# Mixture-of-experts stage: four small moves of work on VectorE, GpSimd and in the buffers

## The chip, the cores and the metric

The kernel runs on one core of a Trainium2 chip. The metric is the device time of one execution in microseconds, the median of several runs. The profile is that of one further execution, taken by the hardware profiler.

## The reference

Three stages follow one another; the output of each is the input of the next. The sizes are 2 batches of 576 tokens, so 1152 tokens of 512 values, all in float32.

```python
# 1. attention, 8 heads of 64, with rotary positions on q and k
scores = (1 / np.sqrt(64)) * np.matmul(q_rot, k_rot.transpose(0, 1, 3, 2))
attn = softmax(scores)                      # over the last axis
x = np.matmul(attn, v)                      # then to (1152, 512)
# 2. dense feed-forward, 512 -> 2048 -> 512
h = x @ w_in
x = np.maximum(0.01 * h, h) @ w_out
# 3. eight experts, 512 -> 1024 -> 512, the two best of each token
logits = x @ w_gate
noisy_logits = logits + np.log1p(np.exp(x @ w_noise)) * noise
top2 = two largest noisy_logits of a token; top2_w = softmax over the two
for e in range(8):
    for k in range(2):
        mask = top2[:, k] == e
        h = np.maximum(x[mask] @ w1[e], 0.0)
        out[mask] += top2_w[mask, k, None] * (h @ w2[e])
```

## The kernel before

The change touches only the third stage. Each expert gets a fixed block of `C` = 320 rows, in three groups of 128, 128 and 64. A branch at the end (`tc.If(crowded > C)`, line 1298) handles an expert with more rows; it is not taken here. Each float32 operand is split into a high half (`fp32r`) and a low half, the rest; a product takes three matmuls: high by high, high by low, low by high. `xe[e]` is the pair of rows of expert e, `xe_h` and `xe_l`, 4 x 320 values in each of 128 partitions.

**Units.** An expert is cut into eight units f of 128 hidden values. A unit is `expert_mm1` (12 matmuls of line 599, then `relu`, lines 1139 to 1141: ScalarE writes the high half `g_x` or `g_y`, VectorE its low half) and `expert_mm2` (eight matmuls, lines 1158 to 1162, into three banks `yr`). The loop runs over n = 8e + f. An iteration first issues `expert_mm1` and `relu` of a later unit (the next one for n below 9, the one after next from then on), then the side work of the unit, then `expert_mm2` of its own unit, then `refill`, which splits two weight blocks for a unit twelve later (lines 217 on ScalarE and 219 on VectorE) and issues the loads of further ones on SyncE. In this stage the order of work on TensorE, VectorE, ScalarE and GpSimd is the order in which the program issues it; each engine works its queue in order.

**From routing to rows.** For expert e, `row(e)` (line 740, VectorE) makes numbers and gates of the tokens, `onehot(e, js)` (line 938, VectorE) makes one-hot columns `hot`, one instruction for each of nine groups of tokens, and `table(e)` (line 950) multiplies the two in nine small matmuls on TensorE. VectorE then makes row numbers and gates of it (lines 958 to 967), and `gather(e)` (line 978) fetches the rows: ten indirect DMAs on GpSimd's queue into the tile `got`. `turn(e, f)` does what follows in four steps at the units that `TURN` gives: `turn_x(e, 0)` turns the first half of `got` on VectorE (line 988) and writes its `xe_h` on ScalarE (line 990), `low_x(e, 0)` writes its `xe_l` on VectorE (line 999), and the same again for the second half. In iteration (e, f) the program works on the rows of expert e + 1 and on `row`, `onehot` and `table` of expert e + 2: `row` at f = 4, columns 0 to 4 at f = 5, columns 5 to 8 at f = 6, the table and the gather at f = 6 too, behind the columns. For e = 0 `row` and the columns come at f = 2 and 3.

**The first expert.** Its rows are not gathered by a table: `rows` (lines 808 to 814) copies the last three blocks of 128 tokens into `x1_row` tiles and stores them to memory by SyncE; 24 matmuls at line 1110 put the expert's rows into four banks `xk`; ScalarE (line 1123) and VectorE (line 1121) write `xe_h` from there, two banks each, VectorE the four pieces of `xe_l` (line 1125), and the `opening` matmuls (line 1233) begin the experts.

**Addresses.** The pool `moe2_x` has two buffers for each name; the first tile of a name gets buffer 0, the next buffer 1, and so on in turn. The pool is laid over memory that has just come free. Counted down from the upper end of a partition, in bytes, buffer 0 of `xe_h` lies at 33,536 to 38,656 and buffer 1 at 28,416 to 33,536. Of what lay there before, `x1` took 12,288 to 30,720, `gx` 30,720 to 36,864 and the three `x1_row` tiles 36,864 to 43,008. A writer of a new tile waits for the users of what lay at its address.

**The end.** `put_y(e, st)` scales a group of an expert's results (`scale_y`) and adds it to `out` by an indirect DMA on GpSimd (`add_y`, line 1191): 24 scatter-adds in all. Those of the last expert stand behind the branch. With the 70 gathers and three of the first expert (line 1036), GpSimd issues 97 indirect DMAs. The program ends (line 1391) when SyncE has waited for all transfers and every engine has run its closing drains.

Of the kernel before, what the change touches and what calls it, by code (L numbers as in the profile page):

```python
# [11 lines left out]
F32R = mybir.dt.float32r  # L12
# [11 lines left out]
E, FF2 = 8, 1024  # L24
# [5 lines left out]
C = 320  # L30
# [50 lines left out]
def f32(t):  # L81
    return t.bitcast(F32)
# [3 lines left out]
def fused_kernel(ctx, tc, q, k, v, w_in, w_out, w_gate, w_noise, noise, w1, w2, consts, out):  # L86
    nc = tc.nc
    V, A, G, T = nc.vector, nc.scalar, nc.gpsimd, nc.tensor

    def pool(name, bufs=1, **kw):  # L90
        return tc.tile_pool(name=name, bufs=bufs, reuse_waits="tile", **kw)
# [231 lines left out]
    def turn(pr, n, a, at=None):  # L323


        r = roped[pr, n][0]
        if pr == 0:
            if at is None:
                p = aside.append(ps_o.tile([128, 1024], F32, name="pT", tag="o")) or aside[0]
            else:  # L330
                p = ps(at, "pT", (128, 1024))
            turned[pr, n, a] = p
            for j in range(KT):
                if a == 0:
                    T.transpose(p[:64, j * 128:(j + 1) * 128], r[:, j, 0], ident)
                else:
                    T.transpose(p[:, j * 128:(j + 1) * 128], r[:, j].rearrange("p h d -> p (h d)"), ident)
            return
        p = ps(at, "pT")
        for j in range(KT):  # L340
            for w in range(2):
                T.transpose(p[:, w, j * 64:(j + 1) * 64], r[here(w), j].rearrange("p h d -> p (h d)"), ident[here(w), here(w)])  # L342
        turned[pr, n, a] = p[:, :, :KT * 64].rearrange("p w (j n) -> p j w n", n=64)
# [394 lines left out]
    def row(e, J=slice(0, NJ), a=0, z=5):  # L738
        n, t = parts(e), row2[e % 2] if e else row0
        V.tensor_tensor(t[:, J, :, a:z], sel[:, J, e, :n, None].to_broadcast([128, J.stop - J.start, n, z - a]),  # L740
                        load[:, J, e, None, a:z].to_broadcast([128, J.stop - J.start, n, z - a]), op=OP.mult)
# [194 lines left out]
    def onehot(e, js):  # L936
        for j in js:
            V.tensor_scalar(hot[e % 2][:, j], iota_32 if e else iota_b, BIG, place[:, j, e:e + 1], op0=OP.add, op1=OP.is_equal)
# [6 lines left out]
    def table(e, bk, a=0, z=5):  # L945

        w, n = z - a, parts(e)
        t = bk[:, :n * w].rearrange("p (a b) -> p a b", b=w)
        for j in range(NJ):
            T.matmul(t, hot[e % 2][:, j], (row2[e % 2] if e else row0)[:, j, :, a:z], start=(j == 0), stop=(j == NJ - 1))  # L950
        whole = nc.allow_low_precision(reason="whole numbers")
        if e == 0:
            with whole:
                V.tensor_reduce(idx[e], t[:, :, 0:2], axis=AX.X, op=OP.add)
            V.tensor_reduce(gates[e], t[:, :, 2:5], axis=AX.X, op=OP.add)
            return
        if a == 0:
            V.tensor_reduce(found[:, 0, :n], t[:, :, 0:2], axis=AX.X, op=OP.add)
            V.tensor_scalar(chunks[e - 1], found[:, 0, :n], 4.0, const("quad"), op0=OP.mult, op1=OP.add)
        if z == 5:  # L960
            V.tensor_reduce(found[:, 1, :n], t[:, :, 2 - a:5 - a], axis=AX.X, op=OP.add)
            m = tmp.tile([128, 2, 3, 4], F32, name="found_here")
            V.tensor_tensor(m, found.rearrange("p w (s q) -> p w s q", q=4),
                            const("mine")[:, None, None, :].to_broadcast([128, 2, 3, 4]), op=OP.mult)
            with whole:
                V.tensor_reduce(idx[e], m[:, 0], axis=AX.X, op=OP.add)
            V.tensor_reduce(gates[e], m[:, 1], axis=AX.X, op=OP.add)
# [4 lines left out]
    got, xe = {}, {}  # L972

    def gather(e):

        got[e] = m2.tile([128, NB32 * 128], F32, name="got", bufs=1)
        for b in range(NB32):
            G.indirect_dma_start(out=got[e][:, b * 128:(b + 1) * 128], out_offset=None,  # L978
                                 in_=x1_rows.rearrange("n (q c) -> (n q) c", q=4),
                                 in_offset=bass.IndirectOffsetOnAxis(ap=chunks[e - 1][:, b:b + 1], axis=0))  # L980
# [119 lines left out]
    for i in range(3):  # L1100
        t = gpool.tile([128, 2 * C + 64], F32R, name="g_x", bufs=3)
# [13 lines left out]
    m2 = m2stack.enter_context(pool("moe2", bufs=2, side="right"))  # L1115
    m2xstack = ExitStack()
    m2x = m2xstack.enter_context(pool("moe2_x", bufs=2, side="right"))
    xe[0] = [m2x.tile([128, 4, C], F32R, name=f"xe_{t}") for t in "hl"]
    for k in range(4):
        if k % 2:  # L1120
            V.tensor_copy(xe[0][0][:, k], xk[k][:, :C])
# [22 lines left out]
    def expert_mm1(e, f, between=None):  # L1144
        h = hb[(8 * e + f) % 3]
        mm1(c0 + 8 * e + f, h, xe[e], 0, C, between)
        return relu(h)
# [3 lines left out]
    def expert_mm2(e, f, g, sts=(0, 1, 2)):  # L1151

        hi, lo = slots[(c0 + 8 * e + f) % NSLOT]
        hi, lo = hi[:, 1], lo[:, 1]
        for st in [st for st in sts if st < 2]:
            gh, gl = (g[:, o + 128 * st:o + 128 * st + 128] for o in (0, C))
            for t, (s, w) in enumerate(((gh, hi), (gh, lo), (gl, hi))):
                T.matmul(yr[st], s, w, start=(f == 0 and t == 0), stop=(f == 7 and t == 2))  # L1158
        if 2 not in sts:
            return  # L1160
        T.matmul(yr[2], g[:, 2 * C - 64:], hi, start=(f == 0), stop=(f == 7), skip_group_check=True)  # L1161
        T.matmul(yr[2][:64], g[:, C - 64:C], lo, start=False, stop=(f == 7), skip_group_check=True)  # L1162
# [35 lines left out]
    def put_y(e, st):  # L1198
        r = scale_y(e, st)
        G.memset(spacer, 0.0)  # L1200
        add_y(e, st, r)
# [4 lines left out]
    def refill(c, most):  # L1206

        for p in range(nxt_part[0], min(2 * c, last_part[0], nxt_part[0] + most)):
            while nxt_part[1] <= p + 5:
                load_part(nxt_part[1])  # L1210
                nxt_part[1] += 1
            convert(p, 4)
            convert(p, 5)
            nxt_part[0] += 1
# [5 lines left out]
    def busiest(bk):  # L1220

        for i in range(NJ - T1 + 1):
            T.matmul(bk[:1, :E], one_b[:, :1], chosen[:, T1 + i] if T1 + i < NJ else chosen0, start=(i == 0),
                     stop=(T1 + i == NJ))
        V.tensor_copy(count, bk[:1, :E])
        V.tensor_reduce(most, count, axis=AX.X, op=OP.max)
# [11 lines left out]
        table(1, bank[1], 0, 2)  # L1238
        gather(1)

    TURN = {1: (4, 5, 5, 6)}

    def turn(e, f):

        for (do, part), at in zip(((turn_x, 0), (low_x, 0), (turn_x, 1), (low_x, 1)), TURN.get(e, (1, 2, 3, 4))):
            if f == at:
# [3 lines left out]
    for n, (e, f) in enumerate(seq[:-3]):  # L1250
        while len(gs) < n + (2 if n < AHEAD2 else 3):
            gs.append(expert_mm1(*seq[len(gs)], second if n == 1 else None))
        if (e, f) == (0, 0):
            r1[7]()
            r1[9]()
            r1[8](1, 0, 2)
            onehot(1, last)
        if (e, f) == (0, 1):
            r1[6]()
            r1[8](1, 2, 5)  # L1260
            r1[8](0)
            onehot(0, last)
        if (e, f) == (0, 2):
            table(1, bank[1], 2, 5)
            table(0, bank[5])
        if e + 1 < E:
            turn(e + 1, f)
        if (e, f) == (0, 7):
            busiest(bank[5])
        if e + 2 < E:  # L1270
            if f == (4 if e else 2):
                row(e + 2)
            for i in range(2):
                if f == (5 if e else 2) + i:
                    onehot(e + 2, range(5 * i, 5 + 4 * i))
        if f == 6 and e + 2 < E:
            table(e + 2, bank[1])
            gather(e + 2)
        expert_mm2(e, f, gs[n])
        if f == 7:  # L1280
            for st in range(3):
                put_y(e, st)
        if n:
            refill(c0 + n + NSLOT, 2 if n > 1 else 4)

    crowded = nc.values_load(most, min_val=0, max_val=NT)
    e = E - 1
# [10 lines left out]
    with tc.If(crowded > C):  # L1298
        with ExitStack() as rest:
# [13 lines left out]
            with tc.For_i(0, E, 1) as e:  # L1313
                n = nc.values_load(nparts[:, bass.ds(e, 1)], min_val=0, max_val=8)
                with tc.If(n > 0):
# [4 lines left out]
                    with tc.For_i(0, n, 1):  # L1320
# [4 lines left out]
                        t = bank[4][:CO, :5]  # L1325
# [68 lines left out]
```

## Time and profile before

| | |
|---|---|
| timed, median of 3 runs | 635.39 us (634.35 to 635.54) |
| the profiled execution's own time | 629.85 us |
| its span, first to last instruction | 628.0 us |
| around the span | 1.85 us |
| TensorE matmuls busy | 601.9 us (96%), 4720 instructions |
| VectorE, ScalarE, GpSimd busy | 428.5, 295.7, 248.8 us |
| mean granted clock of TensorE | 0.993 |

PE is TensorE's matmul, PEld its weight load, DVE VectorE, ACT ScalarE, POOL GpSimd, SP SyncE. Times count from the first instruction. A line such as L599 is the line of the kernel. In a timeline the number in brackets is how long the engine sat idle before the instruction, and who released it; a timeline row can merge several instructions of one kind (x4). An `x` before a number counts instructions.

### The profile page before, as it was taken

What the parts mean: (1) busy time and instruction counts of PE and PEld (TensorE: products, weight loads), DVE (VectorE), ACT (ScalarE), POOL (GpSimd) and SP (SyncE); (2) the same over time, 40 slices, a digit from 0 to 9 for tenths busy, and PEclk for the clock granted to TensorE, in tenths of its full rate; (3) what the DMA queues carried; (4) which work ended last, traced back from release to release, by engine and by line L of the source; (5) the groups of instructions that cost most, each with busy time, mean ns of one, the idle gap of its engine ahead of it and who ended that gap; (6) DMA issues with size and microseconds to landing.
All of it is one profiled execution on the core that took longest, in us unless ns stands there. A gap on an engine that the chain in (4) does not pass through costs nothing.

```text
span 628.0 us, 12453 instructions
## 1 busy us (share of the span) xinstructions
PE 601.9 (96%) x4720; PEld 503.5 (80%) x4721; DVE 428.5 (68%) x902; ACT 295.7 (47%) x605; POOL 248.8 (40%) x248
## 2 busy tenths in 40 slices
PE   8999999999999999999999989999999999999991
PEld 4666767777888888897999888898878787878881
DVE  6987887874998888623577568856666666666411
ACT  2555565765545444322244434554545444445311
POOL 6999898456200000100001007463636464646202
PEclk9999999999999999999999999999999999999997
DMA  6510422322568634902943425475757484748303
GB/s 191 161 42 21 119 64 83 87 83 89 152 201 265 205 116 139 301 1 49 276 111 119 161 50 151 146 198 156 196 157 201 151 206 147 208 147 217 53 5 42
DMA packets 83214, 85.84 MB, mean 137 GB/s; under 512 B 12365, under 2 KB 64973, under 8 KB 83150
## 3 DMA queue, kind: packets, MB, share of 16 engines
q1 hardware_dynamic: 76878, 73.82, 38.0%
q0 software_dynamic: 5392, 10.49, 8.5%
q8 instruction: 38, 0.62, 0.4%
q10 hardware_dynamic: 880, 0.69, 0.4%
q14 instruction: 26, 0.21, 0.1%
HBM read 69.96 MB, written 14.98 MB: 135 GB/s over the span
## 4 chain that ended last, share of the span: by engine, by line
PE 86%; DVE 5%; POOL 2%; issue 2%; DMA 1%; ACT 1%; SPq 0%; POOLq 0%; DVEq 0%; ACTq 0%
PE bank L599 31%; PE bank L608 16%; PE bank L1158 13%; PE pS L418 6%; PE pO L435 6%; PE pM L369 3%; PE bank L1162 2%; PE pO L451 2%; PE bank L1161 2%; POOL got L978 2%; DVE half L381 1%; PE bank L748 1%; PE pT L342 1%; PE bank L1233 1%; PE bank L950 1%
## 5 line engine op out<-in xcount | busy, mean ns | idle before, releaser
L978 POOL DMA_INDIRECT got<-x_rows,chunks x70 | 77.5, 1107 | 115.0 <-issue 76.6
L219 DVE TENSOR_TENSOR wl<-raw,wh 128x512 fp32r<-128x512 f32 x128 | 82.6, 684 | 18.6 <-ACT wh L217 18.6
L599 PE MATMUL bank<-xe_l,wh 128*128 128x320 f32 x248 | 77.0, 310 | 0.8 <-DVE xe_l L999 0.8
L599 PE MATMUL bank<-xe_h,wl 128*128 128x320 f32 x248 | 76.9, 310 | 0.0
L599 PE MATMUL bank<-xe_h,wh 128*128 128x320 f32 x248 | 76.8, 310 | 0.0
L217 ACT ACTIVATE wh<-raw 128x512 fp32r<-128x512 f32 x128 | 74.3, 626 | 0.4 <-DMA raw<-in_moe_w 0.4
L422 ACT ACTIVATE p<-pS 128x576 f32<-128x576 f32 x80 | 49.2, 651 | 40.2 <-PE pS L418 38.7
L1158 PE MATMUL bank<-wh,g_x 128*128 128x512 f32 x192 | 68.1, 395 | 0.0
L620 ACT ACTIVATE g_t<-bank 128x512 f32<-128x512 f32 (+2 forms) x48 | 23.6, 491 | 94.5 <-PE bank L599 93.6
L608 PE MATMUL bank<-g_h,wh 128*128 128x512 f32 (+2 forms) x192 | 65.2, 340 | 0.0
L599 PE MATMUL bank<-xh,wh 128*128 128x512 f32 (+2 forms) x192 | 65.0, 339 | 0.0
L599 PE MATMUL bank<-xh,wl 128*128 128x512 f32 (+2 forms) x192 | 65.0, 338 | 0.0
L608 PE MATMUL bank<-g_l,wh 128*128 128x512 f32 (+2 forms) x192 | 64.8, 338 | 0.0
L599 PE MATMUL bank<-xl,wh 128*128 128x512 f32 (+2 forms) x192 | 64.8, 337 | 0.0
L608 PE MATMUL bank<-g_h,wl 128*128 128x512 f32 (+2 forms) x192 | 64.5, 336 | 0.0
L381 DVE TENSOR_REDUCE half<-pM 128x2 f32<-128x640 f32 x70 | 51.5, 754 | 16.9 <-PE pM L369 16.2
L621 DVE TENSOR_TENSOR g_f<-bank,g_t 128x512 f32<-128x512 f32 (+2 forms) x48 | 26.8, 557 | 46.1 <-ACT g_t L620 45.6
L1139 ACT ACTIVATE g_x<-bank 128x320 fp32r<-128x320 f32 x48 | 21.0, 438 | 73.9 <-PE bank L599 70.2
L1191 POOL DMA_INDIRECT out<-y_row,idx x24 | 40.7, 1694 | 38.2 <-DVE y_row L1172 18.8
L1141 DVE SCALAR_TENSOR_TENSOR g_x<-bank,g_x 128x320 fp32r<-128x320 f32 x48 | 23.4, 488 | 41.0 <-ACT g_x L1140 41.0
L599 PEld LDWEIGHTS bank<-xe_h,wh 128*128 128x128 f32 x248 | 46.8, 189 | 5.7
L599 PEld LDWEIGHTS bank<-xe_h,wl 128*128 128x128 f32 x248 | 46.7, 188 | 2.8
(250 smaller groups left out, 1442.0 us busy)
## 6 DMA issues: line engine op xcount, KB each, us to landing
raw<-in_moe_w SPq DMA_DIRECT2D x128, 256.0 KB
raw<-in_moe_w_in SPq DMA_DIRECT2D x16, 512.0 KB
raw<-in_moe_w_out SPq DMA_DIRECT2D x16, 512.0 KB
inv_sum<-inv_sums SPq DMA_DIRECT2D x16, 144.0 KB
out<-none SPq DMA_DIRECT2D x9, 256.0 KB
VF<-in_v SPq DMA_DIRECT2D x8, 256.0 KB
kept<-wh SPq DMA_DIRECT2D x4, 512.0 KB
kept<-wl SPq DMA_DIRECT2D x4, 512.0 KB
```

The costliest lines, as they stand in the source:

```text
L217: A.activation(hi[:, part], t, AF.Copy)
L219: V.tensor_tensor(lo[:, part], t, f32(hi)[:, part], op=OP.subtract)
L381: V.tensor_reduce(halves[pr, i][:, :, j], p[:, :, :(320, 256)[i]], axis=AX.X, op=OP.max, negate=True)
L418: T.matmul(p[:, a, 0:288], w[here(a)], x[here(a), cols], start=(t == 0), stop=(t == 3))
L422: A.activation(t, scored.pop((pr, j, z))[:, :, 0:288], AF.Exp, scale=0.125)
L435: T.matmul(y[r, z, 0:288], w[:, 32 * c:32 * c + 32], prob[pr, j, z][:, a], start=(j == 0), stop=False, skip_group_check=True)
L599: T.matmul(h[:, :n], w[:, 0, k * 128:(k + 1) * 128], m[:, k, cols:cols + n], start=(i == 0), stop=(i == 11))
L608: T.matmul(b[:, o:o + n], w[:, 1, ds], m[:, :n], start=(first and opens and t == 0), stop=(last and t == 2), skip_group_check=True)
L621: V.tensor_tensor(g[:, :n], h[:, :n], t[:, :n], op=OP.max)
L978: G.indirect_dma_start(out=got[e][:, b * 128:(b + 1) * 128], out_offset=None, in_=x1_rows.rearrange("n (q c) -> (n q) c", q=4), in_offset= ...
L1158: T.matmul(yr[st], s, w, start=(f == 0 and t == 0), stop=(f == 7 and t == 2))
L1191: s = G.indirect_dma_start(out=out, out_offset=bass.IndirectOffsetOnAxis(ap=idx[e][:r.shape[0], st:st + 1], axis=0), in_=r, in_offset=None ...
```

## The change

The rows of the first expert go into the second buffers of `xe_h` and `xe_l`: two tiles `unused` are taken first, and GpSimd writes one element of each. The last step of `turn` for expert 1, `low_x(1, 1)`, is issued at unit 5 instead of 6, right behind `turn_x(1, 1)` and ahead of the unit's weight splits. From e = 1 on, `row` and the one-hot columns come one unit sooner, at f = 3, 4 and 5; the table stays at f = 6. GpSimd gets a drain at unit 3 of the last expert.

```diff
-    xe[0] = [m2x.tile([128, 4, C], F32R, name=f"xe_{t}") for t in "hl"]
+    unused, xe[0] = ([m2x.tile([128, 4, C], F32R, name=f"xe_{t}") for t in "hl"] for _ in range(2))
+    for t in unused:
+        G.memset(f32(t)[:1, 0, :1], 0.0)
...
-    TURN = {1: (4, 5, 5, 6)}
+    TURN = {1: (4, 5, 5, 5)}
...
+        if (e, f) == (E - 1, 3):
+            G.drain()
         if e + 2 < E:
-            if f == (4 if e else 2):
+            if f == (3 if e else 2):
                 row(e + 2)
             for i in range(2):
-                if f == (5 if e else 2) + i:
+                if f == (4 if e else 2) + i:
                     onehot(e + 2, range(5 * i, 5 + 4 * i))
```

## Rows read from the trace of the kernel before

**Rows 1.** The chain of waits from 340 us, shares by line.
```profile
by line: PE bank L599 37.0%; PE bank L1158 27.4%; PE bank L1162 4.5%; PE bank L1161 4.3%; POOL got L978 4.2%; PE bank L608 3.8%; issue 2.0%; PE bank L1233 1.3%; PE bank L950 1.3%; POOL out L1191 1.1%; DMA got<-x_rows,chunks 0.9%; DVE g_x L1
```

**Rows 2.** Stretch, busy us of each engine, clock, DMA share, GB/s.
```profile
440.00:560.00 120.00, 115.00 (x655) 101.18 (x654) 81.47 (x183) 58.30 (x138) 61.47 (x62) 1.00 0.64 180
```

**Rows 3.** TensorE's waits from 340 us: total, times, longest.
```profile
PE bank L950 <- DVE hot L938: 6.3, 5, 1.3
```

**Rows 4.** Timeline, first expert's rows: start, us, what, idle before.
```profile
366.85 1.92 PE L1110 MATMUL bank<-g_x,xl 128*128 128x320 f32 x12
...
369.29 0.77 ACT L1123 ACTIVATE xe_h<-bank 128x320 fp32r<-128x320 f32 x2 [3.38 <-DMA x_rows<-x_row]
...
369.77 0.42 PE L1233 MATMUL bank<-xe_h,wh 128*128 128x320 f32 x1 [1.01 <-ACT xe_h L1123]
...
370.11 1.67 DVE L1125 TENSOR_TENSOR xe_l<-bank,xe_h 128x320 fp32r<-128x320 f32 x4
```

**Rows 5.** Timeline round the second expert's rows.
```profile
395.20 0.84 DVE L988 STREAM_TRANSPOSE got<-got 128x640 f32<-128x640 f32 x1 [0.17 <-DMA got<-x_rows,chunks]
...
396.08 0.74 ACT L990 ACTIVATE xe_h<-got 128x640 fp32r<-128x640 f32 x1 [2.46 <-DVE got L988]
...
396.43 0.40 PE L950 MATMUL bank<-row,hot 128*128 128x50 bf16 x9
...
396.67 0.48 PE L1158 MATMUL bank<-wh,g_x 128*128 128x512 f32 x1
...
397.37 1.29 DVE L219 TENSOR_TENSOR wl<-raw,wh 128x512 fp32r<-128x512 f32 x2 [1.32 <-ACT wh L217]
...
398.58 0.48 DVE L1141 SCALAR_TENSOR_TENSOR g_y<-bank,g_y 128x320 fp32r<-128x320 f32 x1
...
398.98 0.81 DVE L999 TENSOR_TENSOR xe_l<-got,xe_h 128x640 fp32r<-128x640 f32 x1
...
399.85 0.41 PE L599 MATMUL bank<-xe_l,wh 128*128 128x320 f32 x1 [0.79 <-DVE xe_l L999]
...
401.69 0.50 PE L1158 MATMUL bank<-wh,g_y 128*128 128x512 f32 x1
```

**Rows 6.** Timeline round the table of expert 3, one of five alike.
```profile
428.83 0.30 PE L950 MATMUL bank<-row,hot 128*128 128x50 bf16 x5
...
429.67 0.49 DVE L1141 SCALAR_TENSOR_TENSOR g_x<-bank,g_x 128x320 fp32r<-128x320 f32 x1 [1.10 <-ACT g_x L1140]
...
430.07 0.73 DVE L938 TENSOR_SCALAR hot<-iota,place 128x128 bf16<-128x128 bf16 x4
...
430.90 0.48 PE L1158 MATMUL bank<-wh,g_x 128*128 128x512 f32 x1
...
431.10 0.18 DVE L958 TENSOR_REDUCE found<-bank 128x10 f32<-128x20 f32 x1 [0.29 <-PE bank L950]
...
432.33 1.29 POOL L978 DMA_INDIRECT got<-x_rows,chunks  x1 [11.95 <-issue]
```

**Rows 7.** VectorE's timeline in units 4 and 5 of expert 1.
```profile
423.72 0.62 DVE L740 TENSOR_TENSOR row<-sel,load 128x450 bf16<-128x450 bf16 x1
...
426.47 0.90 DVE L938 TENSOR_SCALAR hot<-iota,place 128x128 bf16<-128x128 bf16 x5
```

**Rows 8.** Groups of GpSimd's DMAs; line 1391's drains (ns, start); last scatters.
```profile
L978 POOL DMA_INDIRECT got<-x_rows,chunks x70 | 77.5, 1107 | 115.0 <-issue 76.6
L1191 POOL DMA_INDIRECT out<-y_row,idx x24 | 40.7, 1694 | 38.2 <-DVE y_row L1172 18.8
...
L1391 POOLq DRAIN  x3: 46/113/9648, 617.5 to 627.7; - x3
L1391 SPq DRAIN  x3: 7/7/13, 622.8 to 627.4; - x3
...
613.65 1.56 POOL L1191 DMA_INDIRECT out<-y_row,idx  x1 [18.80 <-DVE y_row L1172]
617.75 1.42 POOL L1191 DMA_INDIRECT out<-y_row,idx  x1 [0.67 <-DVEq L1298]
```

## Prediction

> **What bounds the kernel now.** I read the chain of waits first: from 340 us to the end it runs almost wholly through TensorE, and its longest links are the matmuls of the experts, lines 599 and 1158 [rows 1]. The table of stretches says the same of 440 to 560 us: TensorE is busy 115.00 of 120 us at a granted clock of 1.00, VectorE 81.47, ScalarE 58.30 [rows 2]. What a change is worth here is therefore the time in which TensorE stands still, and what comes after its last matmul. The list of TensorE's waits names 6.3 us in five stops for the one-hot columns `hot` of the tables [rows 3]; the timeline has two more, 1.01 us once for `xe_h` of the first expert [rows 4] and 0.79 once for `xe_l` of the second [rows 5]. All three are touched. After the last matmul the end is set elsewhere, by GpSimd [rows 8], and that is the fourth part.
>
> **First rows in the other buffer.** The first write of `xe_h` waits for the DMA that stores the last `x1_row` tiles: ScalarE sat idle 3.38 us until 369.29 [rows 4]. The reason is an address: buffer 0 of `xe_h` lies over the pool of those tiles, buffer 1 over `x1` and `gx`, which are read long before. With buffer 1 the writers need only the banks. The matmuls that fill these (24 at line 1110) end at 366.85 + 1.92 = 368.77; the banks close one after the other, two matmuls apart, so the first piece of `xe_h` can be written while the last six still run. TensorE can go on at about 368.77 instead of 369.77, which is its whole idle time of 1.01 [rows 4]. What is late next is `xe_l`: four pieces in 1.67 us [rows 4], from about 369.3 to 371.0, wanted from about 12 matmuls after the start on, 370.6 to 371.1. That just fits. The two one-element memsets on the unused buffers now take over the wait for the store (to 369.2); GpSimd has nothing to do until the gather of expert 1, which hangs on TensorE's table and moves forward with it. Bounds: 0, if buffer 1 waits for something too, and 1.01; I take 1.0.
>
> **Second expert's low half.** Today VectorE turns the second half of expert 1's rows at 395.20, ScalarE writes `xe_h` at 396.08 for 0.74, and `xe_l` comes only at 398.98, behind two weight splits and a rectifier's low half, and TensorE waits 0.79 for it [rows 5]. With the step at unit 5 instead of 6, `xe_l` is the next thing in VectorE's queue: it can start when ScalarE is through, at 396.08 + 0.74 = 396.82, and is done by 397.7. TensorE wanted it at 399.85 - 0.79 = 399.06, after the first part at about 398.06. Even if the gather did not move forward at all with TensorE, it is there in time. The price: VectorE then waits for ScalarE with two weight splits and the rectifier's low half `g_y` of unit 7 queued behind it. It stands idle there today too, 1.32 us until the splits at 397.37 [rows 5], so they move by 0.3 only and the low half ends near 399.4 instead of 399.06 (398.58 + 0.48). TensorE takes it up at 401.69 today [rows 5], at 399.9 after both gains: covered, by 0.5 us if nothing of the first part reaches VectorE and by 1.5 if all does. Bounds 0 and 0.79; I take 0.8, since the step stands earliest in the queue.
>
> **One-hot columns a unit sooner.** This is the large term. At each table TensorE runs five of the nine table matmuls at 428.83, then stops; VectorE does a rectifier's low half at 429.67 and only behind it the last four one-hot columns, 430.07 for 0.73, and line 1158 goes on at 430.90: 2.07 us from the first table matmul to the next useful one [rows 6]. The table of expert 2, whose columns are made early already, shows the same nine matmuls without a stop: 396.43 to 396.67, 0.24 us [rows 5]. So each stop costs 2.07 - 0.24 = 1.83 us, more than the idle time listed for it, because the last four matmuls follow the columns one by one. Five tables (experts 3 to 7; five stops in rows 3) make 5 x 1.83 = 9.15 us. The lower bound is the idle time alone, 6.3 us; the upper one 9.15. I take 9.15, by the row of the same operation without a stop.
>
> What hides the moved work: nothing is added, `row` (0.62) moves from unit 4 to unit 3, five columns (0.90) from 5 to 4, four from 6 to 5 [rows 7]. Unit 3 has a turn of `got`, behind which VectorE stands idle for ScalarE as at expert 1, 1.32 us [rows 5], so `row` fills a hole; unit 4 gets 0.3 more than it has, unit 5 less. VectorE is busy two thirds of the stretch [rows 2]. Without that cover a late low half would have to eat a lead of two units of TensorE before a matmul waited. Next in line is the gather: today it starts at 432.33, some 1.2 us after the first reduction of the table at 431.10 [rows 6]. The reduction can then follow the low half directly, at 430.1, so the gather comes 1.0 us sooner, while TensorE comes 1.83 sooner: the gather loses 0.8 us against it, per expert but not adding up, as each expert starts anew from its table. What it has in hand is not in a row of its own; VectorE's only wait for a gather in all experts is the one of 0.17 us at expert 1 [rows 5], so 0.8 us that were missing would first show as such a wait on VectorE, ahead of the lead of two units.
>
> **GpSimd drained in the last expert.** The last three scatter-adds end with a drain on GpSimd's queue that takes 9648 ns, from 617.5 to 627.2, while the other two of its drains there take 46 and 113 ns and SyncE's three 7 to 13 [rows 8]. The last scatter's descriptors are out at 617.75 + 1.42 = 619.17, and SyncE, which waits for the landing of every scatter, comes to its own drain at 622.8 [rows 8]. From 622.85 to 627.17 the core waits for GpSimd's drain alone: 4.3 us. What sets its length no row shows directly. Behind it stand 70 gathers and 24 scatters [rows 8] and three gathers for expert 0 with no drain between: 8.0 us after the last issue over 97 is 0.08 us each (an estimate from these rows). If the drain works off what all of them left, a drain in the last expert leaves three, and the last one ends before SyncE's: gain 4.3. If it is a fixed price after any scatter, the gain is 0. Those are the bounds. I take 4.3, since the two drains that have no indirect DMA before them are the nearest rows to a drain with little behind it. The new drain itself stands behind expert 6's scatters; GpSimd then idles 18.80 us until the last ones [rows 8], so 9.65 us fit, with the register load and branch behind it.
>
> The Trainium skill ("VectorE: DVE Perf Modes", The DRAIN you can't avoid) says that the drains of preamble and postamble take some 12 ns, constant, on all five engines. The row of SyncE agrees (7 to 13 ns); GpSimd's drains differ, this one by a factor of 800. By that rule the 9.65 us would not be the drain's own work, an earlier drain would do nothing, and the sum would be the first rival's.
>
> **The sum.** 1.0 + 0.8 + 9.15 + 4.3 = 15.25 us, made on the profiled execution: 629.85 (span 628.0 and 1.85 around it) becomes 614.6. The timed runs lie 5.5 us above that execution with the same program; I leave that difference as it is: 635.39 - 15.25 = 620.1.
>
> **Rivals.**
> (1) The end stays GpSimd's. The last drain costs the same after three scatters as after 97: for it speaks that no row shows a drain behind only a few indirect DMAs, against it the 46 and 113 ns. The gain is 10.95, the time 624.4.
> (2) Another wait takes the stop's place: the tables still wait for VectorE, now for what stands at the head of its queue, and TensorE goes on only when the low half is through at 430.07 instead of 430.90. The five stops then give 5 x 0.83 = 4.2 instead of 9.15, and the time is 625.1. Against it: the last column is then issued before that low half, and VectorE works in order.
> (3) Slower. The drain in the last expert takes GpSimd beyond its idle time: the last three scatters are queued behind it. It decides from 18.80 us on; to lose the 10.95 us and 1.3 more, the drain would have to last about 31 us, three times the longest that was seen, and the time would be over 636.7. Nothing speaks for it but that a drain in the middle was never seen.
> (4) Buffer 1 of `xe_h`, or the gather of expert 1, waits for something that is hidden now: one or both of the small terms are gone, 621.1 to 621.9.
>
> **How the numbers follow.** Chances: the forecast 0.69, (1) 0.18, (2) 0.06, (4) 0.04, (3) 0.03. The range goes from 618.5 (the forecast less what repeated runs scatter, and a few tenths where the small terms do more) to 625.6, which takes in (1), (2) and (4). Within 0.2%, 1.3 us, is about what a measurement of this kernel cannot tell from no change. Faster by more than that: everything but (3) and a failing of the large term and the drain together, 0.95; the same 0.02; slower 0.03.
>
> **What would show it.** The waits for `hot` gone from TensorE's list and nine table matmuls in about 0.25 us at each expert; the opening matmul of line 1233 with no DMA ahead of `xe_h`, 1 us sooner; `xe_l` of expert 1 right behind its `xe_h` and no wait at line 599; a drain of some 8 us in the idle time of GpSimd near 600 us and a last one so short that SyncE's drain comes last. It would be wrong if TensorE's stops came back under another name (a gather's landing, `g_x`), or if the last drain kept its 8 us.

## The result and the profile after

The changed kernel takes 614.07 us (median of 5 runs, 613.45 to 614.28) beside 635.39 for the kernel before (5 runs, 634.35 to 637.68): a ratio of 0.9651, 95% interval 0.9632 to 0.967. The gain is 21.3 us; forecast were 15.25 and a time of 620.1, and 614.07 lies below the range. The profiled execution tells another story: 614.23 us after, 629.85 before, a gain of 15.6, and the sum made on it said 614.6. The mechanism and the sum held where they were worked out. What failed is the step from the profiled execution to the timed runs.

TensorE's waits from 340 us in the kernel after (total, times, longest); `hot`, `xe_h` and `xe_l` of [rows 3 to 5] are gone, and these two rest, which are there before as well:

```profile
PE bank L1110 <- ACT x_row L808: 0.8, 1, 0.8
PE bank L887 <- DVE chosen L873: 0.2, 1, 0.2
```

The stretch of [rows 2] in the kernel after (busy us of each engine, granted clock, DMA share, GB/s): TensorE is busy 120.00 of 120 us, where it was 115.00.

```profile
440.00:560.00 120.00, 120.00 (x695) 106.49 (x694) 86.32 (x193) 64.55 (x151) 69.44 (x67) 1.00 0.67 190
```

The timeline of the kernel after at the first expert's rows (start, us, what, idle before and releaser), against [rows 4]. ScalarE and VectorE are released by the banks, not by the DMA; line 1235, which is line 1233 before, begins at 368.64 instead of 369.77. The last four matmuls shown, for `xe_l`, take 0.99 us because VectorE's four pieces only just keep ahead of them. The memset on the unused buffer waits for the store in their place.

```profile
366.88 1.92 PE L1110 MATMUL bank<-g_x,xl 128*128 128x320 f32 x12
367.96 1.02 ACT L1125 ACTIVATE xe_h<-bank 128x320 fp32r<-128x320 f32 x2 [2.02 <-PE bank L1110]
...
368.64 0.31 PE L1235 MATMUL bank<-xe_h,wh 128*128 128x320 f32 x1
...
369.25 1.68 DVE L1127 TENSOR_TENSOR xe_l<-bank,xe_h 128x320 fp32r<-128x320 f32 x4
369.36 0.09 POOL L1120 MEMSET xe_h<- 1x1 f32 x1 [22.62 <-DMA x_rows<-x_row]
...
370.40 0.99 PE L1235 MATMUL bank<-xe_l,wh 128*128 128x320 f32 x4
```

VectorE and ScalarE of the kernel after at the second expert's rows, against [rows 5]: `xe_l` at line 999 follows its `xe_h` 0.78 us later and is done by 396.4, ahead of the weight splits and of `g_y`; TensorE has no wait there.

```profile
393.94 0.85 DVE L988 STREAM_TRANSPOSE got<-got 128x640 f32<-128x640 f32 x1
394.81 0.74 ACT L990 ACTIVATE xe_h<-got 128x640 fp32r<-128x640 f32 x1 [2.35 <-DVE got L988]
...
395.59 0.83 DVE L999 TENSOR_TENSOR xe_l<-got,xe_h 128x640 fp32r<-128x640 f32 x1 [0.81 <-ACT xe_h L990]
396.33 1.29 DVE L219 TENSOR_TENSOR wl<-raw,wh 128x512 fp32r<-128x512 f32 x2
...
397.53 0.48 DVE L1143 SCALAR_TENSOR_TENSOR g_y<-bank,g_y 128x320 fp32r<-128x320 f32 x1
```

TensorE and VectorE of the kernel after round the table of expert 3, against [rows 6]: nine table matmuls without a stop, 0.24 us to the next useful one, and the reduction right behind the low half. The unit, from its first matmul of line 599 to that of the next, takes 3.94 us; before it took 5.78 (five alike).

```profile
426.62 0.40 PE L950 MATMUL bank<-row,hot 128*128 128x50 bf16 x9
426.86 0.48 PE L1160 MATMUL bank<-wh,g_x 128*128 128x512 f32 x1
...
427.46 0.49 DVE L1143 SCALAR_TENSOR_TENSOR g_x<-bank,g_x 128x320 fp32r<-128x320 f32 x1 [1.26 <-ACT g_x L1142]
427.87 0.17 DVE L958 TENSOR_REDUCE found<-bank 128x10 f32<-128x20 f32 x1
```

The drains of the kernel after (shortest, median, longest in ns; first and last start in us), against [rows 8]: the new one at line 1273, then GpSimd's and SyncE's at the end (line 1395, 1391 before). GpSimd's longest is 4911 ns instead of 9648 and ends at 611.1. SyncE comes to its drains at 611.6, so the end now waits for SyncE.

```profile
L1273 POOLq DRAIN  x1: 10795/10795/10795, 580.4 to 580.4; - x1
...
L1395 POOLq DRAIN  x3: 46/113/4911, 606.2 to 612.2; - x3
L1395 SPq DRAIN  x3: 7/7/13, 611.6 to 611.9; - x3
```

### The profile page after: what moved, and what is told of

The parts are those of the page before. It is cut to its first block, busy times and chain, and to the rows that moved or that the text cites. A ratio compares the mean times of both kernels' runs of the same rounds, so it can differ in the third digit from the quotient of the medians.

```text
span 612.5 us, 12458 instructions
## 1 busy us (share of the span) xinstructions
PE 598.7 (98%) x4720; PEld 502.0 (82%) x4721; DVE 428.9 (70%) x902; ACT 294.4 (48%) x605; POOL 252.8 (41%) x250
## 4 chain that ended last, share of the span: by engine, by line
PE 93%; DVE 4%; issue 1%; ACT 1%; POOL 1%; POOLq 0%; DVEq 0%
PE bank L599 34%; PE bank L608 16%; PE bank L1160 14%; PE pS L418 7%; PE pO L435 6%; PE pM L369 3%; PE bank L1164 2%; PE bank L1163 2%; PE pO L451 2%; PE pW L532 1%; DVE half L381 1%; PE bank L748 1%; PE pT L342 1%; PE bank L1235 1%; PE bank L1110 1%
## 5 line engine op out<-in xcount | busy, mean ns | idle before, releaser
L978 POOL DMA_INDIRECT got<-x_rows,chunks x70 | 82.2, 1174 | 77.8 <-ACT wh L217 45.1
```

## Experiments

The kernels below were timed in six sets (the first four experiments are the first set), each set on one chip and with the kernel before in it. Ratios are against the kernel before of the same set, with a 95% interval. In the six sets it took 629.93, 629.57, 630.06, 629.83, 632.09 and 629.95 us. A median like the result's 635.39 never came back.

**The kernel before, once more** (no edit).

> The kernel before, unchanged, to see its spans run by run. The profiled execution of before took 629.85 us, its timed ones 634.4 to 637.7; the changed kernel's profiled execution and its timed ones agree (614.2 and 613.5 to 614.3). Theory E (the end): GpSimd's last drain is of varying length, 9.65 us in the profile and some 15 in the others. Theory R (expert 1's rows): the gather of expert 1 lands later in other executions and TensorE waits some 6 us for it instead of 0.8. Theory S (stops): the five stops at the tables are longer in other executions by about 1.1 us each. Theory O: it lies outside what the change touches. All expect spans of some 632 to 634 in most runs and a minority near 628; if the profile falls on a longer one, its extra 5 us stand in the drain (E), ahead of line 599 near 399 us (R), at the tables (S), or elsewhere (O).

629.93 us (629.41 to 630.24, 11 runs), span 628.3. Its profile is [rows 3], [rows 6] and [rows 8] again. No run was of the longer kind, so the four theories are not tested by it. The profiled execution's 629.85 is the usual time of this kernel, and the 5.5 us on top are what has to be explained.

**The drain alone.**

```diff
+        if (e, f) == (E - 1, 3):
+            G.drain()
```

> The kernel before with the drain in the last expert alone. E: 635.4 - 4.2 - 5.5 = 625.7, with spans that no longer vary. R, S and O: 635.4 - 4.2 = 631.2. If the drain is a fixed price after any scatter (rival 1 of the prediction): 635.4.

625.73 us (625.55 to 625.8), ratio 0.9931 [0.9918, 0.9945]: 4.20 less. GpSimd's drains at its end:

```profile
L1393 POOLq DRAIN  x3: 46/113/5002, 617.5 to 623.6; - x3
```

**The columns alone.**

```diff
-            if f == (4 if e else 2):
+            if f == (3 if e else 2):
                 row(e + 2)
...
-                if f == (5 if e else 2) + i:
+                if f == (4 if e else 2) + i:
```

> The kernel before with the one-hot columns a unit sooner alone. S: 635.4 - 9.2 - 5.5 = 620.7. E, R and O: 635.4 - 9.2 = 626.2.

620.8 us (620.15 to 621.27), 0.9853 [0.9838, 0.9869]: 9.13 less, and no wait for `hot`. This time and that of the drain alone agree with a line of their forecasts (S here, E there) by luck: both lines start from 635.4 and take off a hidden 5.5 us, and here the kernel before stood at 629.93, without them. What the two runs show is the terms, 4.20 and 9.13.

**All but the drain** (the change without its `G.drain()`).

```diff
-        if (e, f) == (E - 1, 3):
-            G.drain()
```

> The changed kernel without the drain in the last expert. E: 614.1 + 9.7 = 623.8 and a last drain that varies. R, S: 614.1 + 4.2 = 618.3. O: 614.1 + 4.2 = 618.3, or 5 us more in a part of its runs.

618.75 us (618.08 to 619.1), 0.9821 [0.9808, 0.9834]: 11.18 less, with a last drain of 9650 ns. With the 4.2 of the drain that is 15.4.

**The changed kernel, once more** (no edit).

> The changed kernel unchanged, timed beside the kernel before on one chip, where the kernel before took 629.93 us. Theory B (base): the four terms are as summed, 15.3 us, and only the 635.39 us from which they were taken off is not this kernel's time on this chip: 614.5 and a ratio near 0.976. Theory H (hidden): the kernel before has some 5.5 us more to lose that only part of its executions show, and the changed kernel is free of it: 614.1 against runs of before that reach 634 to 638, ratio 0.965.

614.17 us (613.16 to 614.47) beside 629.57, 0.9751 [0.9738, 0.9764]: 15.4 less, as theory B has it. The kernel after has the time of the result; the kernel before is 5.8 us faster than there.

**The buffer and the low half without the rest**, then **each by itself**.

```diff
-    xe[0] = [m2x.tile([128, 4, C], F32R, name=f"xe_{t}") for t in "hl"]
+    unused, xe[0] = ([m2x.tile([128, 4, C], F32R, name=f"xe_{t}") for t in "hl"] for _ in range(2))
+    for t in unused:
+        G.memset(f32(t)[:1, 0, :1], 0.0)
...
-    TURN = {1: (4, 5, 5, 6)}
+    TURN = {1: (4, 5, 5, 5)}
```

> The kernel before with the other buffer and the sooner low half alone. B: 1.1 + 0.8 = 1.9 us, 628.0 beside 629.9, no wait for xe_h or xe_l on TensorE's list, the five stops for hot and the drain of 9.65 us as before. H, if what is hidden sits at expert 1's rows: as B on a chip where before takes 629.9, but 628 against 635 where it takes that.

> The kernel before with the first rows in the other buffer alone, timed beside the kernel before once more. B (only the base of the sum was off): before near 629.7, this 1.1 us less, 628.6; the wait of 0.8 us for xe_l stays, as gather and TensorE move forward together. H (some executions of before are 5.5 us longer): runs of before at 634 to 638 among these; if what is long sits at the first expert's rows, this kernel has none of it.

> The kernel before with the second expert's low half at unit 5 alone. The prediction's term: 0.8 us less than before, no wait at line 599 for xe_l. A rival: xe_l is not what sets line 599, and the wait moves to another tile with no gain. Base: before near 629.8 (B) or at 634 to 638 (H).

Both: 627.88 us, 0.9969 [0.9958, 0.998], 1.7 less. The buffer: 628.78, 0.998 [0.9971, 0.9989], 1.3 less; the wait for `xe_l` stays at 0.7. The low half: 629.13, 0.9989 [0.998, 0.9998], 0.7 less; that wait is gone and the one for `xe_h` stays at 1.0. Each small term is there by itself; the intervals are wide beside them (0.7 to 1.8 us for the buffer, 0.1 to 1.3 for the low half), and it is the waits that tell them apart.

**The drain earlier**, at unit 3 of expert 4, with 32 indirect DMAs between it and the last drain instead of three.

```diff
-        if (e, f) == (E - 1, 3):
+        if (e, f) == (4, 3):
```

> The changed kernel with its drain at unit 3 of expert 4 instead of the last expert: 32 indirect DMAs (20 gathers, 12 scatters) stand between it and the last drain instead of 3. If the last drain works off what each DMA since the drain before has left (5.0 us past the last landing for 97, so 0.05 each): 1.6 us past the landing, which SyncE's own ten waits cover by 0.6, so 614.1 + 1.0 = 615.1. If any earlier drain makes the last one short: 614.1. If only one in the idle time of the last expert does: 618.4.

614.54 us (614.22 to 615.02), 0.9758 [0.9743, 0.9773]. Its last drains:

```profile
L1395 POOLq DRAIN  x3: 46/113/5852, 606.5 to 612.9; - x3
L1395 SPq DRAIN  x3: 7/7/13, 611.7 to 612.6; - x3
```

The time is 0.4 us above the 614.17 of its set, between two lines of the forecast; the drain's length decides. It lasts 4.9 us behind 3 indirect DMAs, 5.9 behind 32 and 9.65 behind 97: from 32 to 97 it is 3.80 / 65 = 0.058 us for each. The two drains put into the experts fit in as well. The last scatter is still being issued when a drain begins; counted from the end of that issue, the drains end 3.25, 4.19, 6.25, 7.75 and 8.00 us later, behind 3, 32, 65, 94 and 97 DMAs. With 3, most of it is the landing of the last scatter, whose last packet ends 2.75 us after the issue. The drain works off what all of them left; it is no fixed price.

**Single profiled executions** of the kernel before, twice, and the kernel after once more (no edit).

> The kernel before once more, with its profile, in case its runs here are the longer ones. B: 630 and the same rows. H: if 634 to 638, the trace names the place of the extra 5 us.

> The kernel before, one profiled look in the same call. B: 630. H: 634 to 638 with the extra time in a row that can be named.

> The changed kernel beside before on whatever chip this call gets. B: 614.2 beside 629.8. H: 614.2 beside 634 to 638.

629.75 and 629.45 us, and 614.26 (two runs) beside 629.83. None was of the longer kind.

**The 5.5 us: both kernels again, in more runs** (no edit).

> The kernel before, unchanged, on whatever chip this call gets, for its spread alone. B: 629.2 to 630.7 as in the four calls so far (chips 0, 9 and 13). H, or a chip on which it is slower: 634 to 638, with a trace of it.

> The changed kernel on the same chip. B: 614.2. If the chip were a slower one for both: 619. H: 614.2 beside 634 to 638.

Here the kernel before showed a part of it: 632.17 us (629.74 to 633.56, 12 runs) and 632.09 (629.27 to 634.31, 17 runs), each run with its own granted clock, 0.992 at 629.27 and 0.988 at 633.56. Of the 29 runs the six with 0.992 or more took 629.27 to 631.14 us, the four with 0.988 or less 632.75 to 634.21. The kernel after stood at 614.3 (613.75 to 614.85, clock 0.995 to 0.997), 0.9718 [0.9688, 0.9749]: 17.8 us less. And one execution of the kernel before, of 632.28 us, was profiled. The last table's unit and the unit after it, in that execution (columns as in [rows 2]; the granted clock is the third number from the end, 0.84 and 0.87):

```profile
551.91:559.14 7.23, 5.67 (x31) 4.47 (x30) 6.25 (x23) 1.59 (x5) 1.29 (x1) 0.84 0.55 182
559.14:563.25 4.11, 4.11 (x21) 3.69 (x20) 0.77 (x2) 1.24 (x3) 3.18 (x4) 0.87 0.62 178
```

The same two units in the profile of the kernel before's first repeat (an execution of 630.03 us):

```profile
551.59:557.35 5.76, 4.51 (x30) 3.71 (x29) 4.26 (x17) 1.59 (x5) 0.48 (x1) 1.00 0.52 171
557.35:560.98 3.63, 3.63 (x21) 3.21 (x20) 1.27 (x3) 1.24 (x3) 2.72 (x4) 1.00 0.54 156
```

Together 11.34 instead of 9.39 us. TensorE's timeline of the 632.28 us execution shows why: it stops 1.56 us for the columns, and a little later its matmuls take half as long again, 0.63 us at line 1158 instead of 0.40, 0.47 at line 599 instead of 0.31, until 560.2.

```profile
555.61 0.69 PE L950 MATMUL bank<-row,hot 128*128 128x50 bf16 x4 [1.56 <-DVE hot L938]
...
556.45 0.40 PE L1158 MATMUL bank<-wl,g_x 128*128 128x512 f32 x1
...
557.43 0.63 PE L1158 MATMUL bank<-wl,g_x 128*128 128x512 f32 x1
...
559.67 0.47 PE L599 MATMUL bank<-xe_l,wh 128*128 128x320 f32 x1
...
560.20 0.32 PE L599 MATMUL bank<-xe_h,wl 128*128 128x320 f32 x1
```

From 558 to 560 us of that execution the granted clock is 0.50, the lower of its two levels, 1.2 GHz:

```profile
558.00:560.00 2.00, 2.00 (x8) 1.60 (x7) 0.56 (x1) 0.00 (x0) 1.70 (x2) 0.50 0.26 36
```

The columns come late because VectorE does, and VectorE because ScalarE does. Once in each of five experts ScalarE waits long before `g_x`, although its bank was full, each time 9 to 10 us ahead of a table's unit:

```profile
417.58 0.44 ACT L1139 ACTIVATE g_x<-bank 128x320 fp32r<-128x320 f32 x1 [2.94 <-PE bank L1162]
...
448.95 0.44 ACT L1139 ACTIVATE g_x<-bank 128x320 fp32r<-128x320 f32 x1 [2.89 <-remote]
...
480.36 0.44 ACT L1139 ACTIVATE g_x<-bank 128x320 fp32r<-128x320 f32 x1 [2.91 <-remote]
...
511.09 0.44 ACT L1139 ACTIVATE g_x<-bank 128x320 fp32r<-128x320 f32 x1 [2.21 <-PE bank L1162]
...
542.84 0.44 ACT L1139 ACTIVATE g_x<-bank 128x320 fp32r<-128x320 f32 x1 [2.88 <-remote]
```

The last matmuls of these banks ended at 414.45, 445.51, 476.91, 508.33 and 539.39, so ScalarE began 3.13, 3.44, 3.45, 2.76 and 3.45 us later; in the first repeat it begins some 0.1 us later. VectorE takes the lateness up in its idle times. Behind the three of 3.44 and 3.45 us these run out: the low half of `g_x` ahead of the last columns comes without the idle time of 1.10 us that it has in [rows 6], and too late.

```profile
554.91 0.48 DVE L1141 SCALAR_TENSOR_TENSOR g_x<-bank,g_x 128x320 fp32r<-128x320 f32 x1
```

Just these three tables' units are long, 6.11, 6.15 and 7.23 us with stops of 1.57, 1.56 and 1.56; the first and the fourth, behind 3.13 and 2.76, take 5.77 with the usual stop of 1.25. The granted clock fell behind the last of the three alone. With 0.48 for the unit after the last, the excess is 0.34 + 0.38 + 1.46 + 0.48 = 2.7 us; the span is 2.2 longer, the experts having begun 0.4 us earlier there. The last drain takes 9652 ns, as ever, so theory E is out for this execution.

ScalarE is told of a full bank by a semaphore (number 104) that TensorE's matmuls advance. Ahead of the three longest waits its next records in this trace stand at 448.87, 480.27 and 542.76: 0.1 us before ScalarE begins, and more than 3 us after the last matmul's end. In the first repeat nearly all follow it within 0.03 us. So by this trace the signal came late; why, no run shows. The trace also lacks a part of the semaphore records: it has 7726 of them. The profiles of the kernel after that belong to the result (7751) and to this set (7886) lack some too, and all the others have 9236 to 9317.

**VectorE made late on purpose.** Is a late VectorE enough? The first five columns of each table are made again at unit 5, twice or three times, in the kernel before, and three times in the kernel after:

```diff
+            if e and f == 5:
+                for _ in range(2):          # 3 in the other two kernels
+                    onehot(e + 2, range(5))
```

> The kernel before, with the first five one-hot columns of a table made twice more at unit 5 of experts 1 to 5 (the same values again): 10 columns more, 10 x 0.18 = 1.8 us of VectorE ahead of each of the five tables. VectorE has 1.1 us of idle time before the low half of that unit, so the last four columns come about 0.7 us later. Theory H (a late VectorE lengthens the stop, and behind a longer stop TensorE's granted clock falls for some us): stops of about 1.9 us instead of 1.25, 5 x 0.7 = 3.5 us, and behind one to five of them a fall of the clock at about 2 us each: 635 to 643 us, mean clock below 0.99, units behind the tables over 3.63 us. Rival (the lateness costs what it is late and no more): 629.8 + 3.5 = 633.3 us, every table's unit about 6.5 us and the next one 3.62, clock 0.993. Rival (the idle time covers it): 629.8.

> As the run before, with the five columns three times more: 15 columns, 2.7 us, so the last four columns come about 1.6 us later. Theory H: stops of about 2.85 us, 5 x 1.6 = 8 us, and a fall of the clock behind each of the five, at about 2 us: 646 to 650 us, mean clock about 0.98. Rival (lateness alone): 629.8 + 8 = 637.8 us at a clock of 0.993.

> The changed kernel with the same 15 columns more at unit 5 of experts 1 to 5. All nine real columns are issued ahead of the low half of that unit, so TensorE's table has nothing to wait for but the last of them. Theory H: VectorE's lateness reaches no table: 614.3 us (within 0.5), no wait for hot, clock 0.995 to 0.997. Rival (the changed kernel is as sensitive to a late VectorE, only without the stops): 1.6 to 2.7 us per expert more, 622 to 628 us, with a wait of TensorE for hot, g_x or a low half.

Ten columns more: 634.86 us (633.48 to 636.75), 1.0069 [1.0047, 1.0091] against 629.95, at clocks of 0.985 to 0.990. That is near the result's 635.39. (Of the eight runs of the kernel before beside it, one took 632.59 at a clock of 0.989, seven 629.6 to 630.3 at 0.991 to 0.993.) Its stops for the columns, all nearly equal by total and longest:

```profile
PE bank L950 <- DVE hot L938: 7.8, 5, 1.6
```

The five tables' units and the unit after each, in its profile (an execution of 636.75 us, the longest of the five):

```profile
427.30:434.97 7.67, 6.10 (x30) 4.83 (x29) 6.42 (x27) 1.59 (x5) 1.64 (x2) 0.78 0.42 141
434.97:438.60 3.63, 3.63 (x21) 3.21 (x20) 0.76 (x2) 1.24 (x3) 2.72 (x4) 1.00 0.58 192
460.27:467.30 7.03, 5.46 (x30) 4.30 (x29) 6.30 (x27) 1.59 (x4) 1.29 (x1) 0.87 0.46 144
467.30:471.65 4.35, 4.35 (x21) 3.93 (x20) 0.76 (x2) 1.24 (x3) 3.17 (x4) 0.82 0.57 166
493.32:499.51 6.19, 4.62 (x30) 3.78 (x29) 5.79 (x27) 1.59 (x5) 0.49 (x1) 1.00 0.50 160
499.51:503.14 3.63, 3.63 (x21) 3.21 (x20) 1.26 (x3) 1.24 (x3) 2.71 (x4) 1.00 0.54 166
524.80:531.56 6.76, 5.19 (x30) 4.13 (x29) 6.31 (x27) 1.60 (x5) 1.05 (x1) 0.91 0.44 146
531.56:536.16 4.60, 4.60 (x21) 4.20 (x20) 0.75 (x2) 1.24 (x3) 3.38 (x5) 0.76 0.54 157
557.78:563.97 6.19, 4.63 (x30) 3.79 (x29) 5.79 (x27) 1.59 (x5) 0.49 (x1) 1.00 0.49 160
563.97:567.60 3.63, 3.63 (x21) 3.21 (x20) 1.27 (x3) 1.24 (x3) 2.72 (x4) 1.00 0.56 158
```

Two pairs at clock 1.00 take 9.82 us, 0.42 above the usual 9.40: that is the lateness. The other three, in which the clock falls, take 11.30, 11.38 and 11.36. So a fall costs 1.5 us on top, and the five pairs make 6.7; the span is 634.9 against 628.3. My 0.7 us of lateness were 0.42; the fall of the clock, in three of five, was in the forecast. The mean clock counts the falls: 0.993 with none of them in the kernel before, 0.990 with the one in the execution of 632.28 us, 0.985 with the three here.

Fifteen columns more: 642.33 us (641.96 to 643.16), 1.0188 [1.0162, 1.0214], clock 0.980 to 0.982. Now it falls at all five tables; the first and the last pair:

```profile
426.77:435.21 8.44, 6.65 (x30) 5.04 (x29) 7.11 (x32) 1.59 (x5) 1.59 (x2) 0.80 0.37 122
435.21:438.83 3.62, 3.62 (x21) 3.21 (x20) 0.75 (x2) 1.24 (x3) 2.71 (x4) 1.00 0.69 199
...
561.95:569.74 7.79, 6.00 (x31) 4.50 (x30) 7.12 (x32) 1.59 (x5) 1.27 (x1) 0.89 0.39 128
569.74:574.14 4.40, 4.40 (x21) 3.98 (x20) 0.77 (x2) 1.24 (x3) 3.18 (x5) 0.80 0.54 164
```

That is 2.7 to 2.8 us a pair, less than the 3.6 expected (646 to 650). The lateness was 1.3, not 1.6 (line 1158 goes on 5.10 us after the unit's first matmul, 3.84 in the first repeat), which leaves 1.4 to 1.5 for the fall, not 2. The rival, lateness alone, said 637.8, or with 1.3 a table some 636.3.

The kernel after with the same fifteen columns: 618.08 us (617.89 to 618.53), 0.9807 [0.9782, 0.9832]. Neither line of its forecast was right (614.3, or 622 to 628). Its table waits too, because the extra columns go into the tile that the table reads: VectorE's run of 19 columns ends at 427.62, and the last of the table's matmuls follows it. So the kernel after is not immune to a late VectorE, but pays the lateness alone: each unit is 4.7 us, 0.78 above the 3.94; five make the 3.9.

```profile
424.45 3.17 DVE L938 TENSOR_SCALAR hot<-iota,place 128x128 bf16<-128x128 bf16 x19
...
427.02 0.95 PE L950 MATMUL bank<-row,hot 128*128 128x50 bf16 x9
```

The clock of that unit is 1.00, and so is the next one's: the same work added costs 3.9 us there (3.8 over the 614.3 of the set before) and 12.4 in the kernel before.

```profile
425.04:429.76 4.72, 4.66 (x31) 3.72 (x29) 4.65 (x23) 1.59 (x5) 0.00 (x0) 1.00 0.35 116
429.76:433.39 3.63, 3.63 (x21) 3.21 (x20) 2.30 (x7) 1.13 (x3) 2.42 (x3) 1.00 0.64 187
```

## Why the prediction was right and where it was wrong

**The terms of the sum.** First rows in the other buffer: 1.0 forecast, 1.3 measured alone, which its interval does not tell from 1.0; line 1235 begins 1.13 us sooner, and `xe_l` "just fits", with 0.2 us of delay in its last matmuls (0.99 us for four, 0.75 before). Second expert's low half: 0.8 and 0.7. Columns: 9.15 and 9.13; 5.78 - 3.94 = 1.84 us a table, so it was right to count from the first table matmul to the next useful one and not the idle time alone. Drain: 4.3 and 4.20; its price for each DMA, estimated at 0.08 us from all that follows the last issue, is 0.058, as the landing is a part of that time. Together 15.25 forecast; 15.4 and 15.6 in two sets that timed both kernels with the kernel before at its usual time, and 15.6 between the two profiled executions.

**The rivals.** (1), a drain of fixed price, fell with the drain alone and with the drain midway. The Trainium skill ("VectorE: DVE Perf Modes", The DRAIN you can't avoid) gives some 12 ns on every engine for the drains at a program's start and end. By that rule the new drain would have brought nothing; the 7 to 13 ns of SyncE agree with it, GpSimd's longest at the end, 4911 to 9648 ns, does not, and the measurement decides. (2), another wait in the place of the stop: the waits show none. (3): the new drain ran from 580.4 to 591.2, 10.8 us and not some 8, and the last scatters were not due before 602; it did not decide. (4): both small terms came.

**The step that failed** is the one sentence that carried the sum to the timed runs: "The timed runs lie 5.5 us above that execution with the same program; I leave that difference as it is". It put at nothing, without a reason, the chance that this difference is a wait which the change removes. The runs show that it is no price of every version: where the kernel before took 635.39 and 632.09, the kernel after stood at 614.07 and 614.30, and in two other sets at 614.17 and 614.26 beside a kernel before at its usual 629.6 and 629.8. What they show in its place: in an execution of 632.28 us ScalarE, and so VectorE, is late, the stop of 1.25 us at the columns grows to 1.57, and behind a part of such stops TensorE runs for 3 us or so at 1.2 GHz, 1.5 us lost each time. Making VectorE late by ten columns brings 634.86. The kernel after has no such stop to lengthen. If the whole difference was of this kind, 15.6 + 5.5 = 21.1 of the 21.3 us are accounted for.

How far this is shown: that a late VectorE lengthens the stops and that the clock can fall behind them is shown, by one execution that had it unasked and by two kernels that were made so. For the other runs at 632 to 634 the granted clock, which goes down as the time goes up, speaks for the same. That the result's runs at 634 to 638 were of this kind is inferred, since none of them was profiled and their clocks are not on record; by the numbers above it takes three falls (4.5 us) and 1 us of lateness. Two things speak for it: the profile of the kernel after that belongs to the result lacks semaphore records as the one of 632.28 us does, and ScalarE is late in it too, by less:

```profile
474.96 0.44 ACT L1141 ACTIVATE g_x<-bank 128x320 fp32r<-128x320 f32 x1 [2.46 <-PE bank L599]
```

It idles 2.00 us there in another profile of that kernel, of 614.55 us. The wait comes again in the three experts behind, 2.40 to 2.46 us instead of 1.99; no stop of TensorE followed, and the time was 614.23. No kernel with the columns alone, or the drain alone, was run beside a kernel before at 632 or more: that it is the columns, and not another part of the change, which takes the difference away rests on the traces. Open are also what delays the signals to ScalarE, and why three of five stops of equal length were followed by a fall of the clock and two were not.

**The range** was built on the terms and on rivals, with nothing for the 5.5 us themselves. A profiled execution that is 4.5 us faster than the fastest timed run says that something in the program varies by that much, and its place was not known; the time with all of it gone, 614.6, should have been a rival with a chance of its own, beside the 620.1.

## What to carry to other kernels

When the profiled execution and the timed runs of one program differ by more than the runs differ among themselves, the difference is a term of the sum: ask which stall of the profile could be longer in the runs not seen, and forecast both with it and without it. A stop of TensorE can cost more than it lasts, because the clock may fall behind it, and then small delays on another engine ahead of it are multiplied; a table fed a unit early takes that away. A queue with many indirect DMAs on GpSimd is worth a drain where GpSimd idles, since here the last drain paid for all that came since the one before.

## What was not expected of the hardware

The granted clock stayed at 1.00 behind five stops of 1.25 us and fell to 0.50 behind four of eight stops of 1.56 to 1.57 us (and behind all five where the columns came 1.3 us late), costing 1.5 us each. GpSimd's drain grows by 0.058 us with each indirect DMA since the last drain (from 32 to 97 of them), and a drain at unit 3 of expert 4 shortened the last one by 3.8 us, at unit 3 of the last expert by 4.7. In one execution of an unchanged program ScalarE began up to 3.45 us after its bank was full, once in each of five experts, and the trace has the signal for it that late.
